# A linear-attention and gated-FFN kernel: the hand-kept order of 1,427 pieces written anew, with two thirds of the value weights asked for ahead of the first gate weights

## The chip, the cores and the metric

The kernel runs on one NeuronCore of a Trainium2 chip. The metric is the device time of one execution in microseconds (us), the median of several runs. Engine names are those of the profile: PE is TensorE's matmul, PEld its weight load, DVE is VectorE, ACT is ScalarE, POOL is GpSimd, SP is SyncE, which only issues DMAs here. A name with a q behind it (SPq, POOLq) is the engine's instruction queue.

## The reference

A linear attention (8 batches, 8 heads, 576 tokens, head size 64, 128 features) feeds a gated feed-forward layer of 4,608 tokens.

```python
def phi(x):
    proj = np.einsum('bhsd,df->bhsf', x, w_phi)
    proj = proj - np.max(np.abs(proj), axis=-1, keepdims=True)
    return np.concatenate([np.exp(proj), np.exp(-proj)], axis=-1)
q_p, k_p = (phi(q), phi(k))
kv = np.einsum('bhsf,bhsd->bhfd', k_p, v)
z = np.sum(k_p, axis=2)
num = np.einsum('bhsf,bhfd->bhsd', q_p, kv)
den = np.einsum('bhsf,bhf->bhs', q_p, z)[..., None] + 1e-06
x = (num / den)              # then [batch, token, head*64]: 4608 x 512
gate = np.maximum(x @ w_gate, 0.0)   # 512 x 1536
val = x @ w_val
out = gate * val @ w_out             # 1536 x 512
```

## The kernel before

The kernel is written as some 1,427 small pieces ("atoms"). Each piece is a closure with a key, for instance `("kr", b, u)`, and issues a few instructions on one or more engines. A string, `ORDER`, lists the numbers of the pieces; `Atoms.run` walks through it and calls each one. Nothing else sets the order: each engine carries out its own instructions in the order in which the pieces are called, and waits on semaphores where its data or its buffer is not ready. A mark (') behind a number lets the piece take its second choice of engine (an eviction on DVE rather than ACT, or the reverse; a scaling on DVE rather than POOL). A word `z3` is three matmuls on zeros that only keep PE busy.

The pieces, by the names that the text uses:

- `kT`, `qT`, `xT` (line 271): turns of 128x128 blocks on PE; `kTc`, `qTc` (line 284) and `xc` (line 662) copy them from PSUM on DVE or ACT. Only batches 0 and 1 turn k and q on PE, and only batch 0 its x; later ones use DMA transposes (`turn`, lines 292 and 298, and `xd`, line 650, all on SP's queue).
- `kr`, `qr` (line 312): projections with tokens as rows, from 64-row operands; `km`, `qm` (line 319): the largest absolute value by row, on DVE. `qc` (line 549): the projection with features as rows.
- `ke` (line 368) and `qe` (line 567): the exponentials, two activations each on ACT; `kk` (line 379) and `qk` (line 583): small exponentials of the maxima, on ACT, needed before values can be scaled.
- `vs` (lines 328 and 414): the values scaled, on POOL; in the second choice on DVE, with a small copy on ACT (line 409) ahead of it.
- `kv` (lines 486 and 509): k's features times values on PE; `kvc` (line 422): its copy, on ACT, or on DVE in the second choice. In batch 0 one `kv` piece makes two PSUM banks, and so two copies.
- `n` (line 597): numerators and denominators on PE; `nt`, `nu` (lines 616 and 628) combine them on DVE into `u`; `xu` takes a reciprocal on DVE (line 635) and multiplies on POOL (line 642).
- `fv`, `fg` (line 734): the value and the gate half of one FFN step, four matmuls each; `fv` is evicted by ACT or DVE (line 749), `fg` on DVE (line 756). `fo` (line 791): the output matmuls, evicted at line 805 and stored by SP.
- `ld`: loads. q, k of batch 1 and later, and the three weight matrices go out on POOL's queue, the values and the first k on SP's. Value and gate weights come in three parts each (`wv0`..`wv2`, `wg0`..`wg2`, line 243), the output weights in one (line 252).

FFN group 0 (batch 0) starts with 256-column half-steps on its first two token chunks, which need `xc` of chunks 0 and 1. All matmul results share eight PSUM banks; a piece that takes a bank waits until the bank's last reader is done.

Of the kernel before, what the change touches and what calls it, by code (L numbers as in the profile page):

```python
# [22 lines left out]

ORDER = """7 z3 82 92 93 83' 84 87 94 86 8 0 98 102 85 89 90 91 88 103 z1 104 96 97 108 105 95 107 106 z1 112
113 109 99 101 110' 111 122 114 115 123' 124 127 118 116 132 1 117 133 119 120 121 125 100' 128 z1
148 149 129 126 187 10 134 188 151 153 155 137 2 131 156 135 158 160 142 130 196 144 136 200 198
150 154 236 139 141 237 143 140 246 247 157 159 152 29 161 162 226 190 192 54 138 256 257 175 163
194 176 164 165 189 145 147' 191 266 177 146 3 267 193 4 169 170 166 167 171 168 195 199 181 178  # L30
182 321 214 5 172 179 183 180 184 201 197 217 215 11 220 221 218 222 219 208 9 322' 216 173 174'
282 283 223 209 185 186' 202 203 238 227' 210 205 206 204 207 240 211 1092 1093 1094 224 225' 239
1095 1096 324 328 228 229 242 212 213' 1097 326 232 1098 1099 1100 1101 1102' 231 6 1103 1104 1105
1106 1107 230 241 1108 243 268 269 270 271 273 258 274 272 261 248 251 260 249 253 255 254 1109 252
259 263 39 1110' 1111 1112' 264 1113 1114 275 250 233 1115 1116' 1117 290 361 262 363 265 292 365
279 280' 281' 323 327 291 295 293 1118 1119 294 1120' 1121 284 325 288 330 30 51 332 334 234 245
244 235 276 277 329 333 285 287 13 40 278' 289 1122 1123 351 296 1124 335 352 353 309 312 310 311
# [3 lines left out]
347' 32 55 61 371 372 307 308' 16 1134 63 388 398 402 399 391 400 383 385 1135' 1136 389 1137 401  # L41
42 403 1138' 405 393 367 368 369 395 392 394 390 1139 1140 1141 33 1142' 1143 1144' 17 43 424 426
428 384 418 454 458 420 1145 456 1146' 422 1147 1148 460 462 464 465 419 421 423 508 512 509 1149
# [4 lines left out]
502 1163 1164 1165' 534 536 538 564 529 531 523 1166 1167 568 503 570 476 574 566 533 569 571 1168  # L48
573 515 514 516 572 18 1169 1170 535 517 539 528 537 530 488 491 524 492 525 526 527 532 1171' 1172
1173 1174 1175 489 563 66 67 565 20 45 504 34 505 506 69 19 44 1176 1177 493 36 1178' 495 1179 567  # L50
507' 1180' 1181 494 490 590 555 496 497 1182' 593 575 591 68 587 588 589 540 1183 592 594 541 542
# [3 lines left out]
585 586 643 1199 1200 46 72 657 661 659 646 650 647 616 619 1201' 608 648 618 649 651 652 609 1202  # L55
# [3 lines left out]
675 676 716 717 741 1217 672 673 677 718 719 704 705 706 707 708 709 47 1218' 1219 1220 1221 1222  # L59
669 670 721 722 723 671 1223 1224 674 720 724 740 615 1225 1226 683 684 685 756 757 725 746 747 749  # L60
53 766 770 768 678 679 743 759 1227 1228 750 1229 1230' 710 711 712 760 713 758 761 763 714 680 681
# [4 lines left out]
1250' 1251 25 74 78 784 77 836 840 838 75 79 76 1252' 1253 831 832 1254 1255 1256' 1257 833 1258  # L66
814 846 847 848 1259 1260 785 786 828 829 830 787 48 834 835 815 817 818 1261 1262' 1263 800 1264
779 780 819 820 821 822 816 823 24 1265 37 1266 1267 1268 864 865 781 788 789 80 884 885 888 867
854 856 824 1269 1270' 866 1271 1272 887 858 889 868 855 857 849 1273 1274 891 850 851 869 859 900
904 902 874 877 28 894 896 1275 1276' 876 875 879 881 1277 1278 1279' 871 1280' 1281 843 878 886  # L70
880 898 844 845 852 1282 1283 81 895 899 901 903 929 933 1284 931 897 1285 905 1286 1287 964 870
853 930 934 968 890 965 935 937 966 1288' 1289 939 932 967 882 883 1290 872 873 974 978 976 861 936
# [4 lines left out]
1308 962 963 1309' 1310 1010 990 1008 1005 1040 1007 1012 57 1044 1006 1014 1009 991 1311 1042 1312  # L77
1313 1314 1051 1011 1000 1013 1045 1047 1049 1039 992 993' 1015 982 1315' 1043 1041 1316' 1001 1002
1003' 1317 1318' 1319 1320 1321 1322' 1323 1324' 971 972 1325 1016 973' 1023 983 1031 1055 1056
1326' 1024 1052 1327 1057 1025 1053 1054 1328' 1329 1034 1035 1330 1058 1059 1060 1061 1063 1064  # L80
1065 1331 1332 1333 1020 1036 1334' 1032 1033 1017 1018 1019 1021 1022 1062 1069 1335 1026 1027
1336 1337 1338 1028 1029 1030 1066 1067 1068 1339 1340 1070 1071 1037 1038 1074 1078 1075 1079 1072
1073 1077 1341 1342 1343 1344 1345' 1346 1347 1348' 1349 1350 1351' 1352' 1353 1354 1355 1356' 1357
1358' 1076 1080 1087 1359 1084 1085 1088 1089 1360 1361 1362 1363 1364' 1365 1366' 1367 1368' 1369
1086 1081 1082 1083 1090 1370 1371 1372 1091 1373 1374 1375 1376 1377 1378 1379 1380 1381' 1382
1383 1384' 1385 1386 1387' 1388 1389 1390' 1391 1392 1393 1394' 1395 1396 1397 1398' 1399 1400 1401
1402' 1403 1404' 1405 1406 1407 1408' 1409 1410' 1411 1412 1413 1414' 1415 1416 1417 1418 1419
1420' 1421 1422 1423 1424 1425 1426'"""


class Atoms:
# [28 lines left out]
def kernel(  # L120
# [713 lines left out]

    atoms.run(ORDER, keep_busy)
# [28 lines left out]
```

## Time and profile before

| | |
|---|---|
| time, median of 3 runs | 379.88 us (379.76, 379.88, 380.89) |
| span of the profiled execution (first to last instruction) | 377.4 us |
| mean granted PE clock | 0.995 |
| PE, DVE, ACT, POOL busy | 98%, 77%, 56%, 40% of the span |
| matmuls | 3,502 |

Of the profiled execution the page gives the span alone. The median stands 2.48 us above it, for what lies before the first and after the last instruction; sums below are made on the span, and the 2.48 us is added at the end.

How to read it: PE is busy nearly all the time, so what matters is where it is not, and what it waits for there. The timeline merges like instructions that follow each other (x4 is four of them); "us" is then the time from the start of the first to the end of the last, and a bracket is the idle time of that engine just before, with what ended it. Matmuls overlap in their pipeline, so the time from one start to the next is what a matmul costs, and less than the duration of one.

### The profile page before, as it was taken

Reading aid. Unit: us, or ns where it says so; the run is one execution under the profiler, and the core shown is the slowest. Engines: PE = TensorE matmul, PEld = TensorE weight load, DVE = VectorE, ACT = ScalarE, POOL = GpSimd, SP = SyncE. Lnnn points to the kernel's source line nnn. Section 1 sums busy time; section 2 is a strip of 40 time slices with the busy share of each in tenths; the row PEclk is TensorE's granted clock in tenths of the full one; section 3 lists DMA queues with packets and bytes.
Section 4 is the critical chain, followed back from the end, with each engine's and each line's share of the span. In section 5 each row is a group of like instructions: output and inputs, shape, how many; then the busy total and the mean of one; then the engine's idle time right before and its main releaser. Section 6 shows DMA issues by size and latency. Waiting matters only on the chain.

```text
span 377.4 us, 8960 instructions
## 1 busy us (share of the span) xinstructions
PE 368.1 (98%) x3502; PEld 197.4 (52%) x3502; DVE 290.7 (77%) x633; ACT 213.1 (56%) x509; POOL 151.3 (40%) x201
## 2 busy tenths in 40 slices
PE   7789999999999999999999999999999999999996
PEld 4568465546545555464554554465455444444443
DVE  6998999988876799888868886988768927824641
ACT  6997888877687556876765359882740302111101
POOL 5883672488275275901842126933700210000000
PEclk9899999999999999999999999999999999999999
DMA  8999999999489959781289678620410130021004
GB/s 260 205 200 215 233 131 174 219 172 137 89 213 236 165 67 171 144 182 28 59 160 179 96 174 132 130 16 16 128 41 2 29 113 29 2 67 58 2 2 109
DMA packets 87929, 45.10 MB, mean 120 GB/s; under 512 B 55824, under 2 KB 82000, under 8 KB 87888
## 3 DMA queue, kind: packets, MB, share of 16 engines
q1 hardware_dynamic: 60208, 30.42, 37.3%
q0 software_dynamic: 27200, 13.57, 28.8%
q8 instruction: 27, 0.44, 0.5%
q10 hardware_dynamic: 480, 0.56, 0.5%
q14 instruction: 14, 0.11, 0.1%
HBM read 37.78 MB, written 9.44 MB: 125 GB/s over the span
## 4 chain that ended last, share of the span: by engine, by line
PE 92%; ACT 3%; DMA 3%; issue 0%; SPq 0%; DVE 0%; POOL 0%; DVEq 0%
PE pa L734 49%; PE pa L791 25%; PE pa L597 5%; PE pa L312 5%; PE pa L486 4%; PE pa L549 2%; DMA qn<-in_q_dram 2%; ACT qp L567 2%; PE pa L271 1%; PE pa L509 1%; DMA vn<-in_k_dram 1%; ACT kp L368 1%; ACT kv L422 0%; ACT val_sb L749 0%; ACT xT L662 0%
## 5 line engine op out<-in xcount | busy, mean ns | idle before, releaser
L791 PE MATMUL pa<-wo_sb,h 128*128 128x512 bf16 (+2 forms) x444 | 99.9, 373 | 0.0
L734 PE MATMUL pa<-xT,wv_sb 128*128 128x512 bf16 (+1 forms) x400 | 99.3, 370 | 0.1
L734 PE MATMUL pa<-xT,wg_sb 128*128 128x512 bf16 (+1 forms) x400 | 99.3, 370 | 0.0
L756 DVE SCALAR_TENSOR_TENSOR h<-pa,val_sb 128x512 bf16<-128x512 f32 (+1 forms) x112 | 74.6, 669 | 27.2 <-PE pa L734 20.5
L749 ACT CAST val_sb<-pa 128x512 bf16<-128x512 f32 (+1 forms) x67 | 38.1, 575 | 97.1 <-PE pa L734 88.0
L567 ACT ACTIVATE qp<-pa 128x512 bf16<-128x512 f32 x144 | 76.2, 618 | 15.1 <-PE pa L549 14.8
L368 ACT ACTIVATE kp<-pa 128x512 bf16<-128x512 f32 (+1 forms) x152 | 77.4, 605 | 11.1 <-PE pa L312 9.8
L328 POOL TENSOR_TENSOR vs<-vn,ek 128x512 bf16<-128x512 f32 (+1 forms) x68 | 67.4, 1005 | 31.1 <-DMA vn<-in_v_dram 15.2
L734 PEld LDWEIGHTS <-wv_sb 128*128 128x128 bf16 x448 | 41.9, 98 | 44.9 <-issue 1.2
L734 PEld LDWEIGHTS <-wg_sb 128*128 128x128 bf16 x448 | 41.6, 98 | 43.5 <-issue 0.7
L791 PEld LDWEIGHTS <-h 128*128 128x128 bf16 x444 | 40.8, 98 | 44.6 <-issue 0.8
L319 DVE TENSOR_REDUCE mq<-pa 128x4 f32<-128x512 f32 x72 | 46.5, 683 | 10.4 <-PE pa L312 10.1
L319 DVE TENSOR_REDUCE mk<-pa 128x4 f32<-128x512 f32 (+1 forms) x76 | 47.8, 653 | 3.9 <-ACT kp L368 2.3
L642 POOL TENSOR_TENSOR xu<-u,r 128x512 bf16<-128x512 f32 x22 | 22.8, 1041 | 67.4 <-DVE r L635 53.5
L642 POOL TENSOR_TENSOR tT<-u,r 128x512 bf16<-128x512 f32 x14 | 14.6, 1042 | 73.0 <-DVE r L635 41.0
L628 DVE TENSOR_TENSOR u<-pa,t 128x195 f32<-128x195 f32 (+3 forms) x120 | 38.2, 333 | 3.3
L616 DVE TENSOR_TENSOR t<-pa,cq 128x195 f32<-128x195 f32 (+3 forms) x120 | 36.8, 325 | 2.2 <-PE pa L597 1.0
L597 PEld LDWEIGHTS <-qp 128*128 128x128 bf16 x640 | 28.1, 98 | 14.0 <-ACT qp L567 0.9
L749 DVE CAST val_sb<-pa 128x512 bf16<-128x512 f32 (+1 forms) x45 | 30.7, 682 | 4.5 <-PE pa L734 3.0
L597 PE MATMUL pa<-kv,qp 128*128 128x65 bf16 x640 | 31.0, 193 | 0.9 <-ACT qp L567 0.5
L805 DVE COPY out_sb<-pa 128x512 f32<-128x512 f32 x13 | 8.9, 688 | 13.8 <-PE pa L791 13.6
L486 PEld LDWEIGHTS <-kp 128*128 128x128 bf16 x480 | 16.6, 98 | 3.9 <-issue 0.7
(71 smaller groups left out, 278.4 us busy)
## 6 DMA issues: line engine op xcount, KB each, us to landing
vn<-in_v_dram SPq DMA_DIRECT2D x6, 1024.0 KB, 7.3
qn<-in_q_dram POOLq DMA_DIRECT2D x8, 512.0 KB, 8.6
out_dram<-tT SPq DMA_DIRECT2D x16, 256.0 KB, 2.9
out_dram<-out_sb SPq DMA_DIRECT2D x16, 256.0 KB, 2.9
kn<-in_k_dram POOLq DMA_DIRECT2D x6, 512.0 KB, 9.1
wv_sb<-in_moe_w_val_dram POOLq DMA_DIRECT2D x3, 512.0 KB, 10.2
wg_sb<-in_moe_w_gate_dram POOLq DMA_DIRECT2D x3, 512.0 KB, 9.1
wo_sb<-in_moe_w_out_dram POOLq DMA_DIRECT2D x1, 1536.0 KB, 19.5
```

Of the source, the lines that this page charges most:

```text
L319: nc.vector.tensor_reduce(m, some.rearrange("p (c f) -> p c f", f=F), axis=AX.X, op=ALU.max, apply_absolute_value=True,)
L328: eng.tensor_tensor(dst[:, :, s, 0:D], src, ek[:, :, s : s + 1].to_broadcast(list(src.shape)), op=ALU.mult,)
L368: nc.scalar.activation(st["kp"][:, s, 0 : n // 2, par, :], st["banks"][par][:, 0 : n // 2 * F].rearrange("p (a f) -> p a f", f=F), AF.Exp, ...
L567: nc.scalar.activation(x["qp"][:, s, slot].rearrange("p a b -> p (a b)"), st["cols", i][par], AF.Exp, scale=sign,)
L597: nc.tensor.matmul(pn[:, E * (2 * i + s) : E * (2 * i + s + 1)], lhsT=x["qp"][:, s, slot, blk, :], rhs=kv_of(b, lo + i)[:, s, :],)
L616: nc.vector.tensor_tensor(x["t", j][rows, 0:n], ab[:, :, 1], c[:, :, None].to_broadcast([np_, n, E]), op=ALU.mult,)
L628: nc.vector.tensor_tensor(x["u"][rows, lo : lo + n], ab[:, :, 0], x["t", j][rows, 0:n], op=ALU.add)
L642: copy_of(alt, nc.gpsimd, nc.vector).tensor_tensor(x["xu"], x["u"][:, :, 0:D], x["r"].to_broadcast([P, H, D]), op=ALU.mult)
L734: nc.tensor.matmul(ps, lhsT=w[:, dc, P * fi : P * fi + P], rhs=xTs[g][:, dc, lo:hi], start=(dc == 0), stop=(dc == NDC - 1),)
L749: copy_by(copy_of(alt, "ACT", "DVE"))(st["val", n], ps)
L756: nc.vector.scalar_tensor_tensor(st["h2"][:, fi, lo:hi], ps, 0.0, st["val", n], op0=ALU.max, op1=ALU.mult)
L791: nc.tensor.matmul(po, lhsT=st["h2"][:, fi, P * t : P * t + P], rhs=wo_sb[:, fi, c0:c1], start=(fi == 0), stop=(fi == NFC - 1),)
```

## The change

The diff replaces the text of `ORDER` alone. All pieces are the same (one of the six matmuls that only keep PE busy is left out); their order is new nearly everywhere, and some marks are set otherwise. The first line of the string, before and now:

```diff
-ORDER = """7 z3 82 92 93 83' 84 87 94 86 8 0 98 102 85 89 90 91 88 103 z1 104 96 97 108 105 95 107 106 z1 112
+ORDER = """z3 82 83' 92 84 93 85 102 88 103 94 87 7 86 0 z1 104 97 107 96 89 106 8 2 95 105 112 99 98 91 90
...
```

**The first place** is the start of POOL's queue: its loads, and the scalings of batch 0's values between them. Before:

```order
L214 DMA qn<-in_q_dram 128x8x256
L220 DMA kn<-in_k_dram 128x4x576
L243 DMA wv_sb<-in_moe_w_val_dram 128x4x512
L328 TENSOR_TENSOR vs<-vn_109,ek 128x4x64 x2
L414 CAST vs<-ek 128x8
L328 TENSOR_TENSOR vs<-vn_109,ek 128x4x64
L414 CAST vs<-ek 128x8
L328 TENSOR_TENSOR vs<-vn_109,ek 128x8x64
L414 CAST vs<-ek 128x16
L243 DMA wg_sb<-in_moe_w_gate_dram 128x4x512
```

And in the change:

```order
L214 DMA qn<-in_q_dram 128x8x256
L243 DMA wv_sb<-in_moe_w_val_dram 128x4x512
L220 DMA kn<-in_k_dram 128x4x576
L243 DMA wv_sb<-in_moe_w_val_dram 128x4x512
L328 TENSOR_TENSOR vs<-vn_109,ek 128x4x64
L414 CAST vs<-ek 128x8
L328 TENSOR_TENSOR vs<-vn_109,ek 128x4x64 x3
L414 CAST vs<-ek 128x8
L328 TENSOR_TENSOR vs<-vn_109,ek 128x8x64 x2
L414 CAST vs<-ek 128x16
L243 DMA wg_sb<-in_moe_w_gate_dram 128x4x512
```

The first value weights move ahead of batch 1's keys, and the second part of them, which stood behind batch 1's queries, ahead of all scalings and of the first gate weights. Two scalings that DVE did (one of 512 and one of 256 columns) are POOL's now.

**The second place** is the end of batch 0's first half, on ACT and DVE: the exponentials of q and k, and the two copies of the first `kv` piece. ACT before, from the last exponentials of the fifth k item on:

```order
L368 ACTIVATE kp<-pa 128x4x128 x2
L567 ACTIVATE qp<-pa 128x512 x4
L422 CAST kv<-pa 128x260
L368 ACTIVATE kp<-pa 128x2x128 x2
L567 ACTIVATE qp<-pa 128x512 x2
L379 ACTIVATE ek<-mk 128x4 x2
L422 CAST kv<-pa 128x260
```

ACT in the change, from the same place:

```order
L368 ACTIVATE kp<-pa 128x4x128 x4
L567 ACTIVATE qp<-pa 128x512 x4
L379 ACTIVATE ek<-mk 128x8 x2
L379 ACTIVATE ek<-mk 128x4 x2
L368 ACTIVATE kp<-pa 128x2x128 x2
L422 CAST kv<-pa 128x260
L567 ACTIVATE qp<-pa 128x512 x4
```

DVE in the change, over the same stretch (mq_408 and mq_435 are the maxima of q's first and second pair of token chunks; tT are the turned blocks, 1024 wide for q):

```order
L284 COPY tT_296<-pa 128x1024
L319 TENSOR_REDUCE mk<-pa 128x2
L284 COPY tT_327<-pa 128x1024
L319 TENSOR_REDUCE mq_408<-pa 128x4 x2
L319 TENSOR_REDUCE mk<-pa 128x2
L422 CAST kv<-pa 128x260
L319 TENSOR_REDUCE mq_435<-pa 128x4 x4
L284 COPY tT_475<-pa 128x256
L284 COPY tT_484<-pa 128x512
L284 COPY tT_510<-pa 128x512
L319 TENSOR_REDUCE mq_408<-pa 128x4 x2
```

Four small exponentials and two of the last k item now stand ahead of ACT's one `kv` copy; the other copy went to DVE; and DVE now takes all four maxima of q's second pair ahead of the last two of its first pair.

**The third place** is DVE just ahead of the first FFN matmul. Before, from the reciprocal of chunk 1 on (the copies of x are on ACT there):

```order
L635 RECIPROCAL r<-u 128x8
L616 TENSOR_TENSOR t<-pa,cq 128x195
L616 TENSOR_TENSOR t<-pa,cq 128x130
L616 TENSOR_TENSOR t<-pa,cq 128x195
L628 TENSOR_TENSOR u<-pa,t 128x130
L628 TENSOR_TENSOR u<-pa,t 128x195 x2
L284 COPY tT_761<-pa 128x1024
```

And in the change, from the same reciprocal:

```order
L635 RECIPROCAL r<-u 128x8
L616 TENSOR_TENSOR t<-pa,cq 128x195 x2
L628 TENSOR_TENSOR u<-pa,t 128x195
L616 TENSOR_TENSOR t<-pa,cq 128x130
L628 TENSOR_TENSOR u<-pa,t 128x195
L628 TENSOR_TENSOR u<-pa,t 128x130
L628 TENSOR_TENSOR u<-pa,t 128x195
L635 RECIPROCAL r<-u 128x8
L662 COPY xT<-pa 128x4x128
```

One of the two copies of x that the first FFN matmul needs is DVE's now and stands behind eight more operations; the copy of q's turned blocks (tT_761) went to ACT.

More of the change, by code (lines that the diff above doesn't have):

```diff
@@ L31 @@
[L31 to L36, printed above, removed]
@@ L66 @@
[L66 to L71, printed above, removed]
@@ L72 @@
-853 930 934 968 890 965 935 937 966 1288' 1289 939 932 967 882 883 1290 872 873 974 978 976 861 936
[4 rows of a table removed]
[L77 to L86, printed above, removed]
@@ new lines @@
+189 164 4 176 145 191 165 201 3 226 177 202 147' 146 169 193 166 203 181 5 170 11 167 195 171 168
+182 178 214 199 54 172 179 183 180 184 215 217 220 197 321 173 218 216 221 282 219 9 6 185 322' 222
+204 186' 223 174 205 238 208 206 209 207 210 283' 1096 211 1094' 1095 1092' 1093 224 30 227' 242
+212 225' 213' 239 1098' 1097 324 241 228 39 231 240 1102 326 328 230 1100 1099 232 1101 1103 1104
+229 1120 268 248 249 251 272 271 258 270 269 243 1108 261 13 273 250 253 1109 1110 259 1114' 1111
+255 263 264 254 1105 275' 265 262 260 1115 1116' 274 1117 233 1112' 290 244 361 252 234 279 294 323
@@ new lines @@
+585 657 649 616 1200 647 1202 586 618 659 650 619 551 1203 648 1204 1201 661 608 617 609 651 1205
+621 1206 610 22 691 642 663 620 693 652 622 73' 695 626 665 23 1207' 629 627 631 1210' 667 1226 643
+644 628 1214' 630 1212' 1215 668 653 1208 633 1211 645 662 632 698 623 46 700 664 666 1216' 702 624
+625 634 736 692 694 656 696 635 738 1227 740 1213 658 737 614 739 1218 654 660 655' 703 741 1219
+697 669 670 672 675 676 699 1222 671 677 1223 683 673 707 704 674 701 705 1220 1217 1228 718 708
+684 719 678 715 377 709 706 1209 716 56 721 722 1224 47 723 717 720 685 1225 766 746 756 768 747
@@ new lines @@
+875 1275 902 1276' 904 1270' 1277 843 1278 844 845 898 896 878 871 1284' 1279 901 50 889 879 895 80
+870 860 899 929 897 905 933 1286' 1287 931 1282' 903 1302 1285 891' 1280' 881 935 939 964 890 930
+932 966 862 967 1281 27 863 965 880 934 872 1290' 937 1300' 882 968 892 936 873 852 969 893' 974
+938 994 883 940 975 996 1301 941 1283 995 906 910 978 911 976 912 1294 1292 921 977 997 81 1293 998
+907 1291 922 942 943 923 924 1303 925 1288 918 919 999 920 953 908 926 948 1295 945 1296 909 927
+944 979 954 946 959 1298' 949 1297 950 1289 1299 913 971 955 960 1304 961 947 1305 914 1004 1046
@@ new lines @@
+984 951 853 915 1050 1006 980 1307 956 1008 1048 1000 987 916 985 928 986 989 1313 988 1306' 1308
+957 1314 917 958 952 962 1309' 1040 1005 963 1042 991 1010 1315' 1310 990 1007 1012 1311 1014 1009
+981 1011 1013 1039 1045 1001 1041 1015 1312' 992 1044 970 1043 982 983' 1049 1316 972 1330 1317
+1047 1002 973 57 1332' 1003 1318 1320 1333 1016 1338 993 1331 1023 1051 1321 1055 1069 1056 1319
+1017 1057 1070 615 1052 1336 1058 1020 1024 1053 1059 1071 1018 1054 1060 1324' 1322 1019 1323 1066
+1061 1025 1021 1334' 1339 1022 1328' 1034 1028 1031 1063 1064 1325 1337 1026 1067 1035 1335 1329
@@ L91 @@
+1422 1423 1424 1425 1426'"""
 class Atoms:
```

45 lines of the change are left out of this document (27 added, 18 removed), and 31 rows, old and new, of the table ORDER.

## The prediction

> **What bounds the kernel now.** First the table of busy time by stretch, with the stretches cut where PE's share changes.
>
> ```profile
> core 0: us, PE busy (x) PEld busy (x) DVE busy (x) ACT busy (x) POOL busy (x), PEclk, DMA share, GB/s
> 9.30:12.70 3.40, 1.90 (x25) 1.00 (x24) 3.27 (x6) 3.40 (x12) 2.39 (x5) 1.00 1.38 202
> 12.70:16.20 3.50, 3.48 (x54) 2.74 (x55) 3.40 (x8) 3.02 (x11) 3.30 (x5) 0.51 1.22 207
> 16.20:20.00 3.80, 3.02 (x87) 2.01 (x82) 3.67 (x8) 3.80 (x13) 3.01 (x6) 1.00 1.25 205
> 25.00:31.00 6.00, 5.33 (x81) 4.27 (x78) 5.49 (x23) 5.82 (x14) 4.56 (x5) 1.00 1.40 201
> 31.00:37.00 6.00, 5.88 (x67) 4.92 (x65) 5.34 (x13) 4.11 (x10) 1.47 (x2) 1.00 1.26 207
> 37.00:44.00 7.00, 7.00 (x53) 3.54 (x52) 6.45 (x13) 5.71 (x20) 2.75 (x4) 1.00 1.23 254
> 60.00:300.00 240.00, 240.00 (x2342) 127.84 (x2342) 200.23 (x450) 152.93 (x360) 110.35 (x138) 1.00 0.69 121
> ```
>
> From 37 us on PE is busy without a break (240.00 of 240.00 us), at the full clock. All its waiting lies before. There DVE and ACT are full (3.27 and 3.40 of 3.40 us at 9.3, 3.67 and 3.80 of 3.80 at 16.2), and PE waits for them. So the time is: when FFN matmuls, the work that fills PE, can start; then PE's own work; then the last store. A new order can move the first, and can spoil the second; it has little to win there but in how often PE changes its kind of operand. The rows of the FFN's start:
>
> ```profile
> 25.43 0.55 DVE L628 TENSOR_TENSOR u<-pa,t 128x130 f32<-128x130 f32 x2
> 26.02 0.20 DVE L635 RECIPROCAL r<-u 128x8 f32<-128x8 f32 x1
> 26.14 0.79 DVE L616 TENSOR_TENSOR t<-pa,cq 128x195 f32<-128x195 f32 x3
> 26.85 0.82 DVE L628 TENSOR_TENSOR u<-pa,t 128x130 f32<-128x130 f32 x3
> 27.62 0.69 DVE L284 COPY tT<-pa 128x1024 bf16<-128x1024 bf16 x1
> 25.38 2.04 POOL L642 TENSOR_TENSOR xu<-u,r 128x512 bf16<-128x512 f32 x2 [0.44 <-DVE r L635]
> 27.66 0.40 PE L271 MATMUL pa<-ident,xu 128*128 128x128 bf16 x4
> 27.35 1.33 ACT L662 COPY xT<-pa 128x512 bf16<-128x512 bf16 x2
> 28.91 0.60 PE L734 MATMUL pa<-xT,wv_sb 128*128 128x256 bf16 x4
> ```
>
> DVE ends chunk 1's `u` at 25.98; the reciprocal, POOL's product (27.42), the turn on PE (28.06) and ACT's copy (28.68) follow, and the first value half-step starts at 28.91, 2.93 us behind that `u`. I ask what the new order does to the 25.98, then to the 2.93, then to what follows.
>
> **The weights.** The named part is worth nothing. The list of waits has no row in which PE waits for `wv_sb` or `wg_sb`; the load that it waits for longest is q:
>
> ```profile
> PE pa L271 <- DMA qn<-in_q_dram: 0.8, 1, 0.8
> 12.60 1.78 PE L271 MATMUL pa<-ident,qn 128*128 128x128 bf16 x16 [0.75 <-DMA qn<-in_q_dram]
> 18.22 0.91 PE L271 MATMUL pa<-ident,kn 128*128 128x128 bf16 x8
> ```
>
> Moved ahead of batch 1's keys and the gate weights, the value weights push both back by one or two loads; POOL issues them while it waits for the first values. The keys are turned at 18.22 before, some 1 us later in the change (below), behind one load more, about as late; I take nothing, bounds 0 and +1 us. The gate weights are wanted after 29 us.
>
> **DVE's work ahead of chunk 1's `u`.** ACT gets about 2 us less to do ahead of the first FFN matmul (two exponentials of batch 1, a cast, one copy of x and one of `kv` go, a copy of q's turned blocks comes); DVE doesn't, and DVE is what this `u` stands on.
>
> ```profile
> 9.52 0.68 DVE L284 CAST tT<-pa 128x512 bf16<-128x512 f32 x1
> 10.33 0.69 DVE L328 TENSOR_TENSOR vs<-vn,pa 128x512 bf16<-128x512 f32 x1
> 10.94 1.88 DVE L319 TENSOR_REDUCE mk<-pa 128x4 f32<-128x512 f32 x3
> 13.66 0.41 DVE L328 TENSOR_TENSOR vs<-vn,pa 128x256 bf16<-128x256 f32 x1
> 13.99 1.28 DVE L284 COPY tT<-pa 128x1024 bf16<-128x1024 bf16 x2
> 23.16 0.42 DVE L422 CAST kv<-pa 128x260 bf16<-128x260 f32 x1
> 23.50 0.35 DVE L628 TENSOR_TENSOR u<-pa,t 128x195 f32<-128x195 f32 x1
> ```
>
> From start to next start: the two scalings that go are 0.61 (10.33 to 10.94) and 0.33 (13.66 to 13.99). There come a cast of four blocks that ACT did (0.60, like the one at 9.52), the copy of `kv` (0.34, 23.16 to 23.50) and one `t` that now stands earlier (0.79 for three, 0.27). Sum: **+0.27 us**.
>
> **DVE's waits.** Before they come to about 1.4 us, all but 0.26 in three rows, and none after 10.4:
>
> ```profile
> 5.40 0.43 DVE L319 TENSOR_REDUCE mk<-pa 128x2 f32<-128x256 f32 x1 [0.23 <-ACT kp L368]
> 6.37 0.69 DVE L284 CAST tT<-pa 128x512 bf16<-128x512 f32 x1 [0.54 <-PE pa L271]
> 7.76 1.84 DVE L319 TENSOR_REDUCE mk<-pa 128x4 f32<-128x512 f32 x3 [0.37 <-PE pa L312]
> 14.31 1.02 PE L312 MATMUL pa<-w,tT 64*128 64x128 bf16 x12
> 20.04 0.50 PE L312 MATMUL pa<-w,tT 64*128 64x128 bf16 x8
> 17.72 0.41 ACT L422 CAST kv<-pa 128x260 bf16<-128x260 f32 x1
> 17.97 0.72 ACT L368 ACTIVATE kp<-pa 128x256 bf16<-128x256 f32 x2
> 19.47 0.38 ACT L379 ACTIVATE ek<-mk 128x4 f32<-128x4 f32 x2
> ```
>
> In the change the early ones shrink to one of about 1.0: DVE is free at 5.17, the third turn, now ahead of the projection that stood before it, ends near 6.1, and the gap at 7.76 closes. Three new ones come. (1) The copy of the first q turn started at 13.99. Without the two scalings (0.94), with the cast (0.60) and 0.4 less of early waits, DVE gets to it at 13.25. That turn can't start before q lands (12.60 before) and takes half of the 1.78 us, to 13.53: 0.35 us with the hand-over. (2) Next stands the last k item's maximum. PE makes that projection behind the second q turn, at 14.31, so it ends at 14.71, and DVE is free at 14.2: 0.55 us. (3) DVE's third maximum of q's second pair needs a `qr` that takes the bank of ACT's `kv` copy. Before, that copy follows the q exponentials at once (17.72 to 18.13). Now two pairs of small exponentials (0.19 a pair from start to start, 19.47 to 19.66) and the last k item's two (0.54, 17.97 to 18.51) stand ahead: it ends at about 19.05, and the projection (0.50) at 19.6. DVE, from 14.78 on, has two small maxima, a q copy, four large maxima (0.6 each) and the `kv` copy ahead, 4.1 us, and is idle from 18.9: 0.7 us. Sum: 1.6 less the 0.4 saved early, **+1.2 us**. Bounds: +0.3 if (2) and half of (3) are covered, +2 if the third turn gains nothing. So the `u` of chunk 1 ends at 25.98 + 0.27 + 1.2 = 27.45.
>
> **From there to the first FFN matmul.** DVE must now do nine small operations, then copy chunk 0's x itself. Seven such operations took 1.60 us (26.02 to 27.62), 0.23 each; nine are 2.05, and with the copy (0.43, ACT's two take 0.65 each) and the hand-over 2.6 us against 2.93: **-0.3 us**. POOL's way through chunk 1 is no longer than it was. The first FFN matmul starts at about 30.1 instead of 28.91: **+1.2 us**.
>
> **PE's own work behind it.** Each time PE goes between 128-row and 64-row operands it loses about 0.1 us, as two rows show, which differ only in what stands around them:
>
> ```profile
> 235.29 1.73 PE pa L734 x8
> 242.11 1.83 PE pa L734 x8
> ```
>
> The second starts out of a 64-row group. Counting these changes over the whole order gives 86 before and 90 now: **+0.4 us**. Between 28.9 and 37 us PE idled 0.67 + 0.12 us less the 0.48 that fell ahead of 28.9, 0.3 in all, for banks that DVE holds. In the change DVE takes three of the first four value evictions, but PE comes later; I let this go: **-0.3**, bounds -0.3 and +0.5. Further on I cost the edits at nothing: the cover is PE's own queue of FFN work, and DVE's load, 200 of 240 us, is the same. A scaling or an x transposed too late would cost what it is late.
>
> Sum: 1.2 + 0.4 - 0.3 = +1.3 on the profiled span of 377.4, hence 378.7; with the 2.48 us between span and median, **381.2 us**. What a measurement of this kernel can tell from no change is about 0.3%, 1.1 us, so the edge to slower lies at 381.0.
>
> **The rivals.**
>
> *Not later.* The three new waits of DVE are cancelled because PE runs at its full clock from 12.7 to 16.2, where it had 0.51 before. Sixteen turns then take 0.9 us rather than 1.78; the last k projection ends by 13.9, waits (1) and (2) go, and ACT, with 2 us less to do, gets to its `kv` copy sooner. It decides if the stretch before, 9.3 to 12.7, keeps PE busier than 1.90 of 3.40. Start +0.2 (1.2 less the 0.9 of (1) and (2)), changes of operand +0.4, waits -0.3: 380.2, within 0.3%. Less than 0.6 us can be won in all: DVE's work ahead of the `u` isn't less, its waits can't fall below the 1.0 for the first k, and the changes of operand cost 0.4. That speaks against "faster" altogether.
>
> *A second slow stretch.* The row at 12.7 has a granted clock of 0.51 behind a stretch with PE busy 1.90 of 3.40; the row at 16.2, busy 3.02 of 3.80, is followed by the full clock. In the change PE waits for banks between 17.2 and 19.6 and does some 2.2 of 3.4 us, nearer to the first. If the clock halves from 19.6 to 23, the second `kv` piece and what feeds it take about 1.2 us longer: 382.4. The Trainium skill (TensorE: Matmul & The Clock Gate, "What's actually happening") says that the clock is gated by how busy PE was in a free-running window of about 3.4 us, which does not start with the kernel. The stretch of 3.4 us at 0.51 agrees. By that rule where the window falls is chance, and either of these two rivals could differ from run to run.
>
> *Late x.* In group 7 two x transposes now stand on SP's queue behind that of the chunk whose `u` is last. Before, the last was issued at 304.63 and FFN group 7 began at 310.37.
>
> ```profile
> 304.63 1.22 SPq L650 DMA_TRANSPOSE xT<-xu  x1
> xT<-xu SPq DMA_TRANSPOSE x12, 2.5
> 310.37 1.03 PE L734 MATMUL pa<-xT,wv_sb 128*128 128x512 bf16 x4
> ```
>
> With 6.8 us of DVE's work and POOL's two products behind the last `n` of that group, 1.22 us of issue for each transpose and 2.5 to landing, the last would land some 1.8 us ahead of its use, as against 3.2. It costs from the point where DVE is 1.8 us behind there; at 3 us behind, 1.2 us: 382.4.
>
> **How the numbers follow.** Forecast 0.52 (380.4 to 382.0; by its bounds 0.30 of it slower, 0.22 within); not later 0.28 (379.3 to 380.8; 0.05 faster, 0.23 within); second slow stretch 0.12 and late x 0.08, both slower. Faster 0.05, within 0.45, slower 0.50. The range leaves out the best tenth of "not later" and the worst of the last two: 379.3 to 383.2.
>
> **What would show it.** The first FFN matmul in the timeline: near 30.1 (forecast), 29 (not later), 31.3 (slow stretch). DVE's brackets before the q copy, the last k maximum and the third maximum of q's second pair: 0.35, 0.55, 0.7. No wait for `wv_sb` or `wg_sb`. PE without idle time from 40 us on; a bracket "<-DMA xT" there means late x. A first FFN matmul before 28.9 makes the whole prediction wrong.

## The result and the profile after

| | before | after |
|---|---|---|
| time, median | 380.24 us (379.76 to 380.89, 4 runs) | 385.46 us (384.51 to 386.44, 4 runs) |
| ratio, with its 95% interval | | 1.0138 [1.0109, 1.0167] |
| span of the profiled execution | 377.4 us | 383.8 us |
| first FFN matmul | 28.91 us | 30.14 us |
| from the first FFN matmul to the start of PE's last matmul | 344.6 us | 349.7 us |

The changed kernel is slower, by 5.2 us. I forecast slower by 1.3 us, and a range up to 383.2 us; the time lies outside it. (On the three chips of the experiments the kernel before takes 379.4 to 379.6 us, so the runs below are compared by their ratio to it.)

The table splits the span where the prediction did. The first FFN matmul stands at 30.14 us, where 30.1 was forecast. The miss lies behind it. The table of busy time by stretch, for the changed kernel, with the stretch whose row for the kernel before read 240.00 of 240.00 us for PE:

```profile
core 0: us, PE busy (x) PEld busy (x) DVE busy (x) ACT busy (x) POOL busy (x), PEclk, DMA share, GB/s
60.00:300.00 240.00, 234.59 (x2260) 125.07 (x2295) 201.01 (x446) 154.40 (x363) 102.97 (x127) 0.99 0.67 120
155.45:158.85 3.40, 1.06 (x6) 0.39 (x5) 3.37 (x3) 1.03 (x3) 3.14 (x5) 1.00 0.71 168
158.85:162.26 3.41, 3.41 (x27) 1.89 (x26) 3.35 (x6) 1.16 (x4) 0.78 (x1) 0.50 1.36 242
```

PE is no longer full. (About 50 matmul records are missing from this trace, 0.2 us of apparent gap each, so the busy sums are a little low; the waits below are not touched by it.) Within one stretch of 7 us stand a gap of over 2 us and, behind it, 3.41 us at a granted clock of 0.50. The list of PE's waits behind the first FFN matmuls, which was empty before, names the gap:

```profile
PE pa L734 <- DMA xT<-tT: 2.3, 1, 2.3
PE pa L791 <- issue: 0.8, 5, 0.2
PE pa L734 <- ACT kp L368: 0.4, 1, 0.4
PE pa L597 <- ACT xT L662: 0.2, 1, 0.2
```

The first row is the prediction's sign of a late x.

So the 6.4 us of the two spans are: 1.2 at the start, 2.3 waiting for `xT`, 1.7 at half clock (half of 3.41 us), 0.4 in a wait for a bank that ACT holds at 81 us, and 0.8 that no single row shows, of which the changes between 128-row and 64-row operands were forecast at 0.4. The medians differ by 5.2 us only. In every execution whose span is on record the time stands 1.7 to 2.1 us above the span. So of the 2.48 us that the prediction adds between span and median, 0.4 to 0.8 must be that the profiled execution of the kernel before was faster than the median.

**Why `xT` was late.** The half-step that waits is the first of FFN group 3, the x of batch 3. SP's queue, POOL's queue and the chain at that place, in the changed kernel:

```profile
146.54 0.34 SPq L772 DMA_DIRECT2D out_dram<-tT  x1
147.00 2.95 SPq L650 DMA_TRANSPOSE xT<-xu  x2
149.99 1.27 SPq L650 DMA_TRANSPOSE xT<-tT  x1
```

```profile
147.69 1.04 POOL L642 TENSOR_TENSOR xu<-u,r 128x512 bf16<-128x512 f32 x1 [2.98 <-DVE r L635]
148.67 0.95 POOL L214 DMA_DIRECT2D qn<-in_q_dram  x1
149.64 1.06 POOL L328 TENSOR_TENSOR vs<-vn,ek 128x512 bf16<-128x512 f32 x1
```

```profile
149.99 8.01 DMA xT<-tT
158.00 0.14 issue
158.13 2.91 PE pa L734 x8
```

Three transposes stand behind a store on SP's queue, and SP issues the store at 146.54. Two of the three have had their products from POOL since 140.04 and 142.51 us; the one between them waits for the last product of x, done at 148.73, and the last stands behind it. POOL then issues batch 5's queries (512 KB), and the last two transposes go out beside it. The last is issued at 149.99 and takes 8.01 us to land, where a transpose usually takes 2.5. PE had nothing else to do from 155.8 on. In the kernel before, the same load and the same transposes overlapped too, and the landing times show it (the view of line 650 from 135 to 155 us before, and from 135 to 160 us after):

```profile
DMA to landing us min/median/max: 3.0/4.9/6.8
```

```profile
DMA to landing us min/median/max: 2.5/6.9/8.0
```

But before, the last of them was issued at 147.19 and group 3 began at 153.68, 6.5 us later, and the one that took 6.8 us was issued at 139.67. In the new order the slow ones are the last ones.

**What stands right behind.** DVE and POOL from 152 to 159 us, in the changed kernel:

```profile
153.63 2.25 DVE L328 TENSOR_TENSOR vsm<-vm,ek 64x512 bf16<-64x512 f32 x2
155.80 2.69 DVE L395 CAST vsm<-ek 64x16 bf16<-64x16 f32 x1
158.52 0.69 DVE L319 TENSOR_REDUCE mq<-pa 128x4 f32<-128x512 f32 x1
```

```profile
152.82 2.51 POOL L328 TENSOR_TENSOR vs<-vn,ek 128x512 bf16<-128x512 f32 x2 [2.12 <-ACT ek L379]
156.23 1.06 POOL L328 TENSOR_TENSOR vs<-vn,ek 128x512 bf16<-128x512 f32 x1
157.23 0.26 POOL L414 CAST vs<-ek 128x16 bf16<-128x16 f32 x1
157.38 1.04 POOL L328 TENSOR_TENSOR vs<-vn,ek 128x512 bf16<-128x512 f32 x1
```

One of the marks that the change sets makes DVE, not POOL, scale half of the mixed values of batches 4 and 5 (line 328, then a cast of 16 columns, line 395). That cast takes 2.69 us, where POOL's take 0.25, and it ends as POOL's last product does. DVE is held for 4.9 us, and the q maximum behind it releases a bank. In the changed kernel this hides behind the wait for `xT`; the experiments bring it out.

### The profile page after: what moved, and what is told of

It is laid out like the page before. It is cut to its first block, busy times and chain, and to the rows that moved or that the text cites. A ratio compares the mean times of both kernels' runs of the same rounds, so it can differ in the third digit from the quotient of the medians.

```text
span 383.8 us, 8876 instructions
## 1 busy us (share of the span) xinstructions
PE 368.2 (96%) x3450; PEld 197.8 (52%) x3501; DVE 294.2 (77%) x641; ACT 216.6 (56%) x514; POOL 144.7 (38%) x190
## 4 chain that ended last, share of the span: by engine, by line
PE 86%; DMA 5%; ACT 3%; DVE 3%; issue 2%; SPq 0%; POOL 0%; DVEq 0%; POOLq 0%; ACTq 0%
PE pa L734 47%; PE pa L791 21%; PE pa L597 5%; PE pa L486 4%; PE pa L312 4%; DMA qn<-in_q_dram 2%; PE pa L549 2%; DMA xT<-tT 2%; PE pa L271 1%; ACT kp L368 1%; ACT qp L567 1%; DMA vn<-in_k_dram 1%; DVE t L616 1%; DVE u L628 1%; DVE mq L319 1%
## 5 line engine op out<-in xcount | busy, mean ns | idle before, releaser
L791 PE MATMUL pa<-wo_sb,h 128*128 128x512 bf16 (+2 forms) x426 | 98.2, 373 | 1.4 <-issue 0.8
L734 PE MATMUL pa<-xT,wv_sb 128*128 128x512 bf16 (+1 forms) x384 | 95.5, 374 | 3.2 <-DMA xT<-tT 2.3
L734 PE MATMUL pa<-xT,wg_sb 128*128 128x512 bf16 (+1 forms) x384 | 93.7, 370 | 1.3 <-ACT kp L368 0.4
L328 POOL TENSOR_TENSOR vs<-vn,ek 128x512 bf16<-128x512 f32 (+1 forms) x66 | 66.2, 1016 | 27.0 <-ACT ek L379 23.8
L734 PEld LDWEIGHTS <-wv_sb 128*128 128x128 bf16 x448 | 41.1, 98 | 45.8 <-issue 5.0
L642 POOL TENSOR_TENSOR xu<-u,r 128x512 bf16<-128x512 f32 x20 | 20.8, 1041 | 68.7 <-DVE r L635 51.5
L628 DVE TENSOR_TENSOR u<-pa,t 128x195 f32<-128x195 f32 (+3 forms) x120 | 37.4, 331 | 2.2
L642 POOL TENSOR_TENSOR tT<-u,r 128x512 bf16<-128x512 f32 x13 | 13.5, 1041 | 59.5 <-issue 32.4
L486 PE MATMUL pa<-vs,kp 128*128 128x65 bf16 x384 | 17.5, 196 | 0.0
```

The source lines that it names most:

```text
L328: eng.tensor_tensor(dst[:, :, s, 0:D], src, ek[:, :, s : s + 1].to_broadcast(list(src.shape)), op=ALU.mult,)
L486: nc.tensor.matmul(kv_ps[:, hh, s, :], lhsT=lhsT, rhs=rhs, start=(n == 0), stop=(n == 19))
L628: nc.vector.tensor_tensor(x["u"][rows, lo : lo + n], ab[:, :, 0], x["t", j][rows, 0:n], op=ALU.add)
L734: nc.tensor.matmul(ps, lhsT=w[:, dc, P * fi : P * fi + P], rhs=xTs[g][:, dc, lo:hi], start=(dc == 0), stop=(dc == NDC - 1),)
L791: nc.tensor.matmul(po, lhsT=st["h2"][:, fi, P * t : P * t + P], rhs=wo_sb[:, fi, c0:c1], start=(fi == 0), stop=(fi == NFC - 1),)
```

## The experiments

Twelve kernels. All leave the pieces as they are and change their order or marks; one adds matmuls on zeros. The numbers in the strings are those of `ORDER`.

| kernel | median us | ratio to before, 95% interval | first FFN matmul | from there to PE's last | PE's longest wait behind 37 us |
|---|---|---|---|---|---|
| before | 379.4 to 379.6 | 1 | 28.91 | 344.6 | none |
| changed | 385.46 | 1.0138 [1.0109, 1.0167] | 30.14 | 349.7 | 2.3 for xT |
| q5_early | 383.48 | 1.0093 [1.0062, 1.0125] | 30.63 | 347.5 | 1.8 for DVE |
| mix_on_pool | 384.83 | 1.0114 [1.0075, 1.0154] | 30.27 | 350.4 | 3.1 for xT |
| both | 383.35 | 1.0083 [1.0048, 1.0119] | 29.49 | 347.5 | 1.9 for POOL |
| three | 381.57 | 1.0057 [1.0036, 1.0077] | 29.47 | 345.6 | 0.4 for ACT |
| filler | 383.98 | 1.0116 [1.0102, 1.0130] | 29.82 | 348.3 | 0.4 for ACT |
| start_new_rest_old | 380.81 | 1.0025 [1.0005, 1.0044] | 30.27 | 345.0 | none |
| start_old_rest_new | 383.60 | 1.0102 [1.0069, 1.0136] | 29.13 | 349.9 | 2.3 for xT |
| both_start_old | 382.90 | 1.0078 [1.0047, 1.0109] | 29.66 | 347.9 | 1.9 for POOL |
| weights_only | 381.20 | 1.0041 [1.0017, 1.0065] | 31.70 | 344.8 | none |
| first_third_only | 379.52 | 0.9999 [0.9989, 1.0009] | 28.58 | 344.7 | none |
| both_weights_old | 382.93 | 1.0075 [1.0041, 1.0110] | 30.34 | 347.6 | 1.9 for POOL |
| mix_dve_in_old | 388.63 | 1.0256 [1.0209, 1.0302] | 29.40 | 353.5 | 4.4 for DVE |

The two columns on the FFN are of one profiled execution each. The first FFN matmul of one order moves by over 1 us from execution to execution (the start of the changed order: 29.47 to 30.63 in the seven kernels that keep it, loads included). The length behind it stays within 0.4 us where the order there is the same (both, both_weights_old and both_start_old: 347.5, 347.6, 347.9).

### Start or rest

```diff
-the new order throughout
+start_new_rest_old: the new order up to the first FFN half-step, then what is left in the old order
+start_old_rest_new: the old order up to the first FFN half-step, then what is left in the new order
```

> The changed order up to the first FFN half-step, and behind it all that is left in the order before. Theory A: the start costs the 1.2 us that it showed (first FFN matmul at 30.1 instead of 28.9) and nothing later is late: 380.2 + 1.2 = 381.4 us, between 381.0 and 381.9. Rival: the loss of the changed kernel comes from its start (a late first FFN, loads that are late from there on): 384 or more. Second rival: FFN work takes the start's delay up, 380.2.

> The order before up to the first FFN half-step, and behind it all that is left in the changed order. Theory A: only the start's 1.2 us are won back; group 3's x is late as in the changed kernel, by its wait of 2.3 us or up to 1.2 more since its FFN work comes that much earlier, and the clock halves behind it: 385.2 - 1.2 = 384.0 us, between 383.3 and 385.2. Rival (the start carries the loss): 380.2 to 381.

Measured: 1.0025 and 1.0102. The new start costs 0.95 us, near the 1.2 forecast, and behind it the old order runs its 345.0 us without a wait. The old start does not save the new order: 349.9 us behind the first FFN matmul, the same wait of 2.3 us for `xT`, and a stretch at half clock behind it. Most of the loss is in the rest: by its ratio this kernel is 3.9 us above the kernel before, where 384.0 - 380.2 = 3.8 was expected. (Its interval overlaps that of the changed kernel.)

### The load beside the transposes

```diff
 641 1197
+22
 72 612 577
...
 1206 610
-22
 691 642
```

Number 22 is the load of batch 5's queries, 72 a scaling on POOL of mixed values.

> The changed order, with one atom moved: the load of batch 5's queries (512 KB, on POOL's queue) is asked for ahead of POOL's scaled mixed values, some 6 us earlier, when the DMA engines stand idle, and no longer beside the last two x transposes of FFN group 3. Theory A (late x): the loss beyond my forecast is PE's wait of 2.3 us for that group's x, which landed 7 to 8 us after its issue because of this load, and the half clock for 3.41 us behind it, 1.7 us; both go: 385.2 - 4.0 = 381.2 us, between 380.6 and 382.0, no row of PE waiting for xT and the full clock to the end. Rival B (x late because DVE and POOL made its products late, or because SP's queue held it): the load has nothing to do with it, 384.9 to 385.5, the wait stays. Rival C (the slow stretch of the clock is chance and not tied to the wait): the wait goes, a stretch at 0.5 stays, 382.9.

The wait for `xT` went, and with it the half clock; all four transposes of the group landed by 153.0 us:

```profile
150.48 1.27 SPq L650 DMA_TRANSPOSE xT<-tT  x1
xT<-tT SPq DMA_TRANSPOSE x1, 2.5
```

SP issues the last one 119.85 us behind the first FFN matmul in both kernels (150.48 less 30.63, and 149.99 less 30.14). Only its landing changed, from 8.0 to 2.5 us, so it is the load and not a late product or SP's queue. But only a third of the loss came back: 1.0093. The list of PE's waits from 100 us on has another row in its place:

```profile
PE pa L486 <- DVE mq L319: 1.8, 1, 1.8
```

PE waits for a bank whose reader is the q maximum behind the cast of 2.7 us. Theory A had the cause of the late `xT` right and its reach wrong: a second block stood right behind.

### The mixed values back on POOL, alone and together

```diff
-693 652 622 73' 695 626
+693 652 622 73 695 626
```

Number 73 is the second half's mixed values. "both" has this edit and the one above.

> The changed order, but the scaled mixed values of the second half of batches 4 and 5 (two products and a cast, 4.94 us on DVE in the changed kernel) are made by POOL again, as before the change. The load of batch 5's queries stays where the change put it. Theory A (two blocks at one place, the late x ahead of the busy DVE): PE still waits for group 3's x until about 158, so little is won: 4.2 to 5.2 us above the kernel before, and the stretch at half clock stays. Rival B (DVE's 4.94 us is the cause, and the late x only its trace): the wait for xT goes, 1.0 to 2.0 us above the kernel before.

> The changed order with both moves: the load of batch 5's queries asked for earlier, and the mixed values of the second half of batches 4 and 5 on POOL. Theory A: the two blocks at 155 us are all that the changed kernel loses beyond its start and its extra changes of operand; PE has no wait of over 0.5 us behind the start, the clock stays full: 1.2 to 1.8 us above the kernel before. Rival B: a third wait stands behind the two (POOL now late with its scaled values, or ACT), 2.5 us or more above.

Alone, the wait for `xT` stays, 3.1 us in the profiled execution, with half clock behind it, and the kernel is 4.3 us above the kernel before (1.0114), as theory A had it. Together, the kernel was not 1.2 to 1.8 us above the kernel before but 3.1 (1.0083): rival B, a third wait. The two lists of PE's waits from 100 us on, of mix_on_pool and of both:

```profile
PE pa L734 <- DMA xT<-tT: 3.1, 1, 3.1
```

```profile
PE pa L486 <- POOL vs L414: 1.9, 1, 1.9
```

The `kv` products of batch 4's third pair stand right behind the second half-step of group 3, and POOL has not scaled their values. That is the work of the second move: POOL's two products and a cast for the mixed values now stand ahead of the scaling that PE waits for. The rows of POOL in both (the last one is what PE waits for, from 156.86 us on):

```profile
154.29 2.06 POOL L328 TENSOR_TENSOR vsm<-vm,ek 64x512 bf16<-64x512 f32 x2
158.43 0.24 POOL L414 CAST vs<-ek 128x16 bf16<-128x16 f32 x1
```

And in q5_early, where DVE makes the mixed values, the same cast on POOL, and PE at the same `kv` products:

```profile
157.72 0.26 POOL L414 CAST vs<-ek 128x16 bf16<-128x16 f32 x1
159.76 0.29 PE L486 MATMUL pa<-vs,kp 128*128 128x65 bf16 x4 [1.75 <-DVE mq L319]
```

There POOL is done at 157.98 us, just as PE comes to them at 158.01. So at this place the mixed values make something late on either engine: on DVE the q maximum, for which PE waits 1.8 us, on POOL the scaled values, for which it waits 1.9.

### The third one

```diff
-1226 643 644 628 1214' 630 1212' 1215 668
+1226 643 628 1214' 630 1212' 1215 644 668
```

Number 644 is that `kv` piece; 1214, 1212 and 1215 are half-steps of group 3. Only three FFN half-steps stand between the old and the new place (two value, one gate), not the four that the text on record counts.

> As the kernel with both moves, and in addition the kv products of batch 4's third pair stand three value half-steps and one gate half-step later in the order, behind FFN work of group 3 that is ready. In the kernel with both moves PE still waited 1.9 us there, for POOL's scaled values. Theory A (three chains, those of x, of the mixed values and of batch 4's scaled values, end 2 to 3 us late at one place, and each alone costs about 2 us): that wait goes, 0.8 to 1.6 us above the kernel before, and from the first FFN matmul to PE's last it takes 345.5 to 346.0 us (344.6 before, 349.7 in the changed kernel). Rival B (DVE, ACT or POOL is behind for good from there on): PE's next consumer waits in its place, the time stays within 0.5 us of the kernel with both moves.

The wait goes, as theory A had it. PE's list from 100 us on holds nothing longer than the gaps of missing records:

```profile
PE pa L791 <- issue: 0.8, 5, 0.2
```

From the first FFN matmul to PE's last it takes 345.6 us, within what was expected. The median is 2.1 us above the kernel before (1.0057), more than the 1.6 expected. The profiled execution itself took 380.78 us, 1.3 above; why the median lies higher is not shown. Of theory A's three chains only two are separate: that of x, and that behind the mixed values. The third, batch 4's scaled values on POOL, is late because the mixed values came back to POOL ahead of them; this edit covers that wait with FFN work.

### Idle PE and the half clock

```diff
-627 631 1210' 667
+627 631 z9 1210' 667
```

> The changed order with nine matmuls more (zeros into a bank of their own, 128x512, 0.22 us each) ahead of FFN group 3's first half-step, where PE waits for x. They change no result and no other engine's work. Theory A (the clock halves because PE was idle in the stretch before): the wait for xT shrinks to under 0.7 us since the fillers stand in it, x lands when it did, and no stretch at 0.5 follows: 1.5 to 2.0 us below the changed kernel, 3.0 to 3.7 above the kernel before. Rival B (the half clock has nothing to do with the wait): the stretch at 0.5 stays, 4.7 to 5.5 above the kernel before.

PE and the clock at that place, in the kernel with fillers (the first table is the timeline, the second the busy time by stretch):

```profile
155.32 2.11 PE L200 MATMUL pa<-zeros 128*128 128x512 bf16 x9
157.74 1.02 PE L734 MATMUL pa<-xT,wv_sb 128*128 128x512 bf16 x4 [0.32 <-DMA xT<-tT]
158.96 1.02 PE L734 MATMUL pa<-xT,wv_sb 128*128 128x512 bf16 x4 [0.20 <-DVE mq L319]
```

```profile
155.36:158.77 3.41, 3.08 (x14) 1.16 (x13) 3.38 (x3) 0.80 (x2) 2.93 (x5) 1.00 0.80 181
158.77:162.19 3.42, 3.23 (x33) 1.81 (x33) 3.42 (x7) 1.40 (x5) 1.01 (x2) 1.00 1.38 235
```

`xT` lands at 157.6, as it did; PE is busy meanwhile, and the stretch at 0.50 is gone. So in this pair of executions idle PE is what halved the clock. The gain is smaller than theory A's: 348.3 against 349.7 us behind the first FFN matmul, 1.4 where 1.7 was expected; 0.20 of it is the next half-step's wait for DVE. The ratio is 1.0116 against 1.0138, with intervals that overlap, and by it the kernel is 4.4 us above the kernel before, where 3.0 to 3.7 was expected. The trace speaks for theory A, the time alone would not.

### The weights

The loads on POOL's queue in their order (q of batch 0, k and q of batch 1, q of the mixed tokens; the scalings between them left out), in the order before, in weights_only and in first_third_only:

```diff
-qn kn wv_sb wg_sb qn wv_sb qm wg_sb wv_sb wg_sb
+qn wv_sb kn wv_sb wg_sb qn qm wv_sb wg_sb wg_sb
```

```diff
-qn kn wv_sb wg_sb qn wv_sb qm wg_sb wv_sb wg_sb
+qn wv_sb kn wg_sb qn wv_sb qm wg_sb wv_sb wg_sb
```

> The order before with the weight loads alone in the new order (the first third of the value weights ahead of batch 1's keys, the second behind them and ahead of the first gate weights, the last ahead of the second gate third). Forecast: no change, 380.2 us, between 379.8 and 380.6, since no wait for weights stood in the trace and the keys were not the last that the start waited for. Rival: batch 1's keys land a load later and the start is held by them: +0.5 to +1.0 us, a wait for kn in front of the turns of batch 1's keys.

> The order before with the first third of the value weights ahead of batch 1's keys; the other weights where they stood. In the kernel with all weights in the new order the keys of batch 1 landed 2.5 us later and its queries 2.9 us later, PE waited 2.4 us for the queries, and it took 1.6 us more. Theory A (the queries of batch 1 carry it, pushed back by the second value third): here they land as before, 0.0 to 0.4 us above the kernel before. Rival B (the keys carry it): 1.0 to 1.8 us above.

The forecast fell: 1.0041, 1.6 us, and its rival named the wrong load. PE's list of waits from 20 us on in weights_only, and the timeline at that wait:

```profile
PE pa L271 <- DMA qn<-in_q_dram: 2.4, 1, 2.4
```

```profile
26.73 1.03 PE L271 MATMUL pa<-ident,qn 128*128 128x128 bf16 x8 [2.39 <-DMA qn<-in_q_dram]
```

It is batch 1's queries, which land at 26.69 us instead of 23.75, that PE waits for, not its keys. The first third alone, which pushes only the keys back, costs nothing: 0.9999 [0.9989, 1.0009]. In the profiled execution of weights_only the granted clock was 0.50 from 25.76 to 32.59 us, and its first FFN matmul came 2.8 us later than in the kernel before. How much of the 1.6 us is the wait and how much the clock isn't separated.

The reverse in the new order, in the kernel with both moves:

```diff
-qn wv_sb kn wv_sb wg_sb qn qm wv_sb wg_sb wg_sb
+qn kn wv_sb wg_sb qn wv_sb qm wg_sb wv_sb wg_sb
```

> As the kernel with both moves, but the weights are asked for as before the change: batch 1's keys ahead of the first value third, batch 1's queries ahead of the second, so that the keys and the queries land some 2.5 us earlier. Theory A (the load order costs what it did alone, 1.6 us): 0.0 to 0.4 us above the kernel before. Rival B (in the new start DVE's chain binds and the later load hides beside it): the same as the kernel with both moves, 1.2 to 1.8 above, and the first FFN matmul at 30.0 to 30.6.

As rival B has it, the time is that of both, 1.0075 against 1.0083, and the first FFN matmul stands at 30.34; both lie some 3 us above the kernel before, not 1.2 to 1.8, with the 1.9 us that PE waits for POOL. The trace agrees that the later queries are hidden: in both, PE waits nowhere for `qn` behind 20 us. That DVE's later chain is what hides them (the `u` of chunk 1 ends 1.1 us later in the changed kernel) is argued, not shown.

### The old start under the mended rest

```diff
-both: the new order up to the first FFN half-step
+both_start_old: the old order up to the first FFN half-step, then what is left of "both"
```

> As the kernel with both moves, but up to the first FFN half-step in the order before. Theory A: the start's 1.2 us come back, the changes of operand (0.4 us) and PE's wait of 0.4 us at 81 us stay: 0.2 to 0.8 us above the kernel before. Rival B: the rest of the new order is worth something by itself: 0.3 us or more below the kernel before. Rival C: an FFN that starts 1.2 us earlier meets x or banks that are not ready, so that nothing is won against the kernel with both moves: 1.2 to 1.8 above.

Not settled by its time, which lies 3.0 us above the kernel before and outside all three: 1.0078 against 1.0083, and the first FFN matmul at 29.66 and 29.49 in the two profiled executions. This one had a stretch at half clock from 13.9 to 17.3 us, the other none. The wait of 1.9 us for POOL stays and covers what the start may have won. None of the kernels beats the one before.

### DVE beside a busy POOL

```diff
-80
+80'
...
-81
+81'
```

> The order before, with the scaled mixed values of batches 6 and 7 (both halves; four products of 64x512 and two casts of 64x16) made by DVE where POOL made them. Theory A (a DVE instruction with its operands in SBUF alone waits while POOL works there): beside POOL's row of three scaled values and cast the second pair takes over 1 us for a product and the cast up to about 3 us, ending with one of POOL's instructions; the first pair, where POOL stands still ahead of it, 0.5 to 0.7 us for a product. Rival B (this form is slow on DVE by itself): 1.16 us a product and 2.7 us a cast in both places. The time: 0 to 2 us above the kernel before.

DVE and POOL in that kernel, around the two pieces:

```profile
227.84 1.29 DVE L328 TENSOR_TENSOR vsm<-vm,ek 64x512 bf16<-64x512 f32 x2 [4.04 <-DMA vm<-in_v_dram]
229.06 0.19 DVE L395 CAST vsm<-ek 64x16 bf16<-64x16 f32 x1
244.82 2.37 DVE L328 TENSOR_TENSOR vsm<-vm,ek 64x512 bf16<-64x512 f32 x2
247.12 1.05 DVE L395 CAST vsm<-ek 64x16 bf16<-64x16 f32 x1
```

```profile
245.15 3.96 POOL L328 TENSOR_TENSOR vs<-vn,ek 128x512 bf16<-128x512 f32 x3
249.06 0.25 POOL L414 CAST vs<-ek 128x16 bf16<-128x16 f32 x1
```

Theory A. With POOL at rest two products take 1.29 us and the cast 0.19. Beside POOL they take 2.37 and 1.05, and POOL's three products take 3.96 us where the same three take 3.06 in the kernel before. (The cast stayed below the 3 us expected: it waits for one product of POOL.) The time, 1.0256, is 9.7 us above, far more than the 0 to 2 expected, and not for that reason: the first piece waits 4.04 us for its load and holds all of DVE behind it. PE waits 4.4 us for a copy, and its clock halves:

```profile
227.77:231.18 3.41, 0.12 (x4) 0.12 (x4) 3.33 (x7) 0.00 (x0) 0.00 (x0) 1.00 0.19 39
231.18:234.59 3.41, 3.41 (x12) 1.02 (x10) 2.70 (x7) 2.38 (x9) 2.06 (x3) 0.50 0.22 79
```

In the kernel before, POOL makes these values at 228.56 us, and PE has no wait there.

## Why the prediction was wrong

**The start: right in its sum, by luck.** DVE's three new waits, and the `u` of chunk 1, in the changed kernel:

```profile
14.16 0.69 DVE L284 COPY tT<-pa 128x1024 bf16<-128x1024 bf16 x1 [0.31 <-PE pa L271]
15.35 0.42 DVE L319 TENSOR_REDUCE mk<-pa 128x2 f32<-128x256 f32 x1 [0.49 <-PE pa L312]
19.65 1.29 DVE L319 TENSOR_REDUCE mq<-pa 128x4 f32<-128x512 f32 x2 [0.22 <-PE pa L312]
26.57 0.55 DVE L628 TENSOR_TENSOR u<-pa,t 128x130 f32<-128x130 f32 x2
```

The first two, forecast at 0.35 and 0.55, are 0.31 and 0.49. The third, forecast at 0.7, is 0.22. ACT's `kv` copy ended at 19.21 us, not sooner than the 19.05 forecast; it is DVE that was later, free at 19.43 and not at 18.9. So `u` ends at 27.12, not 27.45. From there to the first FFN matmul it took 3.0 us, not 2.6. The two errors cancel, and since one order's start moves by over 1 us between executions, the agreement of 30.14 with 30.1 is luck.

The rival "not later" had its condition and not its result. In this execution the clock from 12.70 to 16.20 us was full, where it had been 0.51:

```profile
12.70:16.20 3.50, 2.83 (x31) 2.33 (x31) 2.70 (x6) 2.75 (x8) 3.48 (x6) 1.00 1.23 207
13.09 1.89 PE L271 MATMUL pa<-ident,qn 128*128 128x128 bf16 x16 [0.48 <-DMA qn<-in_q_dram]
```

The sixteen turns of q took 1.89 us all the same, not the 0.9 that this rival counted on, and the first two waits stood.

**"The weights. The named part is worth nothing."** Right for this kernel, and for a reason that the prediction does not give. It goes by the gate weights and batch 1's keys. What the second third pushes back is batch 1's queries, and in the old order those were nearly late: 1.6 us when this edit is made alone. In the new start nothing waits for them.

**Changes of operand, +0.4, and waits from 28.9 to 37 us, -0.3.** Nothing contradicts the first: with the waits at 155 us mended, 345.6 - 344.6 = 1.0 us remains behind the first FFN matmul, of which 0.4 is the wait at 81 us and 0.6 is open. The runs do not separate it further. The second was too large: in the 8 us behind the first FFN matmul PE was idle for 0.16 us before and 0.05 us in the changed kernel, 0.1 us less.

**"Further on I cost the edits at nothing: the cover is PE's own queue of FFN work, and DVE's load ... is the same."** This step failed. The three edits, one on top of the other, brought the length behind the first FFN matmul from 349.7 us to 347.5 (the load moved), 347.5 again (the mixed values back on POOL) and 345.6 (the `kv` piece moved): 4.1 of the 5.1 us. The cover was an average over 240 us. At one place, 155 us, PE had no FFN work that was ready, because FFN group 3 itself waited. The load on DVE as a sum is the same (201.01 against 200.23 us), and still one piece of 4.9 us was put onto DVE there. The edits count as nothing only where the work that they delay isn't wanted at once; here x and the mixed values were.

**The late-x rival had the mechanism, and the wrong place and price.** It was given for group 7 with 0.08, at 1.2 us. It came in group 3, at 2.3 us, and with the second slow stretch behind it (the other rival, which I had placed at 19.6 us as a thing by itself): 4.0 us together. Its price rested on "2.5 to landing", the median of that row. The same view of the kernel before has a longest landing of 6.8 us, and that one belonged to group 3, beside the load of batch 5's queries. With 8 us to land instead of 2.5, a lead of 6 us is late. The prediction goes by how far each transpose stands ahead of its use, and takes the landing as a constant.

## What to carry to other kernels

When an order is made anew, check each chain against its first use at that place, and not against the mean load: take the longest landing of a transfer, not the median, and list what else goes out on the DMA queues beside it. A mark that moves a piece to another engine moves its waits there too, and all that is queued behind it waits along. And a wait taken away shows the next one: two pieces were late at one place, so mending the one that the profile names brought back a third of the loss. Moving the second piece to the other engine moved the wait along with it; what took the wait away was other work for PE in the meantime.

## What the runs showed of the hardware

- **DVE and POOL block each other** when both work on SBUF operands alone. A cast of 16 columns on DVE took 0.19 us beside a resting POOL, 1.05 behind one, and 2.69 beside POOL's product, cast and product. A product of 64x512 took 0.65 and 1.19 us (1.29 and 2.37 for two). Nearly all other DVE work of this kernel has an operand in PSUM; in the kernel before, the q maxima beside the same three products of POOL took their usual 0.68 us. The Trainium skill (SBUF — State Buffer, "Who interferes with whom") says that DVE and GpSimd share a pair of ports, that an instruction of DVE with two SBUF inputs contends with one of GpSimd that reads SBUF, and that beside a copy or cast of DVE in a two-port mode whichever issues first holds the pair for its whole instruction. The products and the 1.05 us agree; the 2.69 us span three instructions of POOL, more than one. In which mode the cast ran no run shows.
- **A transpose by DMA lands in 2.5 us, or in 8.0 beside a 512 KB load**, in one FFN group of the changed kernel; with that load issued some 6 us earlier (q5_early) the same transpose landed in 2.5.
- **PE's clock halves for 3.41 us behind a stretch of 3.41 us in which PE was idle for much of the time**, also in the middle of a kernel at full work: behind 1.06 us of busy PE in the changed kernel and 0.12 in the last experiment, not behind 3.08. The Trainium skill (TensorE: Matmul & The Clock Gate, "What's actually happening") has the free-running window and gives an idle window as what halves the clock; here windows far from idle did (1.90 of 3.40 us busy at the start of the kernel before). Where the limit lies stays open: in the kernel both_start_old a stretch with 1.55 us of busy PE, by the same view, was followed by the full clock:

```profile
157.24:160.65 3.41, 1.55 (x25) 0.99 (x24) 1.53 (x3) 2.85 (x8) 3.34 (x6) 1.00 0.92 185
160.65:164.07 3.42, 3.42 (x18) 1.47 (x15) 2.07 (x3) 0.52 (x2) 2.98 (x5) 1.00 1.48 161
```
